# A gated attention and state-space backward pass: pool reuse waits per tile, a reordered lead-in of the channel loop, and gradient sums finished in their own tiles

## The chip, the cores and the metric

The kernel runs on one core of one Trainium2 chip. A core has five instruction streams: TensorE (PE, with its weight loads shown apart as PEld), VectorE (DVE), ScalarE (ACT), GpSimd (POOL) and SyncE (SP). SP computes nothing here: it only issues transfers, and SPq in the profile is its stream of such issues; ACT and POOL issue some too. The metric is the time of one execution on the device in microseconds (us). A run is compared by the median of its executions, and a profile is one more execution, taken with the hardware profiler on.

## The reference

The forward function mixes two branches of the same input x (2048 tokens, 576 channels) with a gate per token, and the reference returns its output and the gradients of all twelve differentiable inputs (everything but B_u):

```python
g = sigmoid((x * gate_w).sum(-1, keepdims=True))
a = softmax(q @ k.T * 18**-0.5) @ v @ wo          # 32 heads of 18, q,k,v = x @ wqkv
K = real(sum_n C * exp(dt*A*l) * (dt*B))          # per channel, 128 states, l = 0..2047
b = causal_convolution(x, K) + x * Dskip          # written with FFTs of length 4096
out = g * a + (1 - g) * b
out, vjp = jax.vjp(f, ...);  grads = vjp(grad_out)
```

So the kernel must compute attention forwards and backwards, a long convolution for each of 576 channels forwards and backwards (with the gradients of A, B, C, log_dt and Dskip), and the products that join them.

## The kernel before, in words

The program is one straight-line trace in five stages, each with its own pools of tiles:

- **Stage 1** (lines 116 to 335): loads, the q, k and v products into a DRAM tile `QKV_d`, the gradient of the attention output `dO_d`, and the parameters of the convolution `par_d`. Its last work is 160 products `ps_dO` and a row of `par_d` stores on the SP queue.
- **Attention** (lines 429 to 828). 8 groups of 4 heads, and in each 4 blocks b of 512 queries: 32 units of 32 steps, with 39 steps more at the end (`OFF`) because the backward part of a unit follows its forward part by 39 steps. A step G issues two exponentials of 128x1024 on ACT (`PT` for the forward part, `eb` for the backward part), two products `ds` of 128x512 on DVE, and on PE the score products and one burst of a gradient: V, Q and K in turn, eight steps to a round. One PSUM bank, `accB`, takes every burst and every turning of a `ds` tile (`turn`, line 553, whose eviction at line 563 is on DVE). The sums over query blocks stay in SBUF: `dvacc` and `dkacc` (four each), and `dqa`. The last addition of a sum goes to a bf16 tile `gb` (`grad_tile`, two buffers), which `store_grad` (line 529) turns with a transposing DMA on the SP queue into `gT` (two buffers); POOL packs it into `dtk` and stores it. In the last block of a group nine sums end so: four of V, four of K, one of Q. In the other blocks only the one of Q does. POOL also computes the basis `E_d` of the convolution in the gaps. The order on all engines is the order of the code (`manual_schedule`).
- **Lead-in of the channel loop** (lines 829 to 1137): tiles, constants, and the first two blocks of channels.
- **The channel loop** (lines 1138 to 1187): 18 blocks of 32 channels. For a block: `m_load`, `m_part`, `m_skw`, `m_sum`, `m_fin` form the products of short lag through a DRAM tile `Md_d` that is read back skewed; `load_en`, `turn_e` and `uv` make `UV` from the basis; `prep_rx` prepares the reversed input `RX`; `k0` and `t0_load` make the kernel's first part through a DRAM tile `Kp_d`; `scan` is the recurrence over 15 pieces on DVE, 43 dependent instructions; `rw1`, `rw2`, `t0`, `ybp` give the output; `pairs1`, `pairs2`, `sums` the parameter gradients. In iteration i, DVE scans block i while PE and ACT prepare block i + 1, and parts of blocks i + 2 and i + 3. Here PE, ACT, DVE and POOL keep the order of the code, and SP's order is chosen by the planner when the program is built.
- **Final stage** (lines 1189 to 1397): the weight gradients `ps_dwq` (320 products), the parameter gradients of the convolution (`emit_dn`), 16 token tiles with `ps_a` and `ps_dx`, and `ps_dwo`. The planner orders all of it.

A tile pool that takes over memory of an earlier pool must wait until the earlier user is done. In the kernel before this is asked of the pool as a whole: the first use of any of its tiles waits for the last use of the earlier pools that it overlaps. Within a pool, a tile of the same tag waits for the buffer that it takes.

The lines that the change touches in the lead-in:

```python
for i in range(-1, NBLK):     # 1138: iteration -1 belongs to the lead-in
    cur = i >= 0
    sb = i + 2 if i + 2 < NBLK else None
    if sb is not None:
        m_skw(sb)
```

Of the kernel before, what the change touches and what calls it, by code (L numbers as in the profile page):

```python
# [11 lines left out]
BF = mybir.dt.bfloat16  # L12
F32 = mybir.dt.float32
# [4 lines left out]
P = 128  # L18


def build(tc, aps, dbg_aps=None, stages=("s1", "attn", "post", "s4", "final")):
    nc = tc.nc
# [39 lines left out]
    with ExitStack() as gctx:  # L62
# [366 lines left out]
        if "attn" in stages:  # L429
# [5 lines left out]
            with ExitStack() as ctx:  # L435
                ctx.enter_context(tc.manual_schedule(engines={mybir.EngineType.PE, mybir.EngineType.Activation, mybir.EngineType.DVE, mybir.EngineType.Pool, mybir.EngineType.SP}))
                ga = ctx.enter_context(tc.tile_pool(name="ga", bufs=2))
                ptp = ctx.enter_context(tc.tile_pool(name="ptp", bufs=41))
                work = ctx.enter_context(tc.tile_pool(name="awork", bufs=2))
                apsp = ctx.enter_context(tc.tile_pool(name="aps", bufs=1, space=bass.MemoryType.PSUM))  # L440
                ident_f = work.tile([P, P], F32, tag="ident_f", bufs=1, name="ident_f")
# [84 lines left out]
                def grad_tile():  # L526
                    return work.tile([P, KB], BF, tag="gb", bufs=2, name="gb")

                def store_grad(gb, g, which, t0):
                    c0 = which * D + g * 4 * DH  # L530
                    gT = work.tile([P, TPQ, 4, HP], BF, tag="gT", bufs=2, name="gT")
                    nc.sync.dma_start_transpose(out=gT.rearrange("p t a b -> p t (a b)"), in_=gb)

                    def pack():
                        dtk = work.tile([P, TPQ, 4, DH], BF, tag="dtk", bufs=1, name="dtk")
                        nc.gpsimd.tensor_copy(dtk, gT[:, :, :, 0:DH])
                        nc.gpsimd.dma_start(dqkv_d[:, t0:t0 + TPQ, c0:c0 + 4 * DH], dtk.rearrange("p t a b -> p t (a b)"))
                    packs.append((now[0] + 4, pack))
# [14 lines left out]
                def turn(tiles, outs):  # L553

                    pt_ = apsp.tile([P, len(tiles), TPQ, P], BF, tag="accB", name="turn_p")
                    for x, t_ in enumerate(tiles):
                        for qb in range(TPQ):
                            nc.tensor.transpose(pt_[:, x, qb, :], t_[:, qb * P:(qb + 1) * P], ident_bf)  # L558

                    def ev():  # L560
                        x = 0
                        for n, o_ in outs:
                            nc.vector.tensor_copy(o_(), pt_[:, x:x + n])  # L563
                            x += n
                    return ev
# [31 lines left out]
                def dv_half(g, b, kq, h, acc):  # L597
                    U = UN[(g, b)]
                    for ii in (2 * h, 2 * h + 1):
                        for j in range(4):  # L600
                            mm(acc[HP * j:HP * (j + 1), :], lhsT=U["dOa"][:, ii, j, :], rhs=U["eb"].pop((kq, ii, j)),
                               start=(ii == 0), stop=(ii == 3), tile_position=(0, HP * j))

                    def ev():
                        if b == 0:
                            DKV[("v", g, kq)] = work.tile([P, KB], F32, tag="dvacc", bufs=4, name="dvacc")
                            nc.vector.tensor_copy(DKV[("v", g, kq)], acc)
                            return
                        a_ = o_ = DKV[("v", g, kq)]
                        if b == NQ - 1:  # L610
                            o_ = DKV[("v", g, kq)] = grad_tile()
                        nc.vector.tensor_tensor(o_, a_, acc, op=A.add)  # L612
                    return ev
# [19 lines left out]
                def dk_half(g, b, kq, h, acc):  # L633
# [7 lines left out]
                    def ev():  # L641
# [5 lines left out]
                        if b == NQ - 1:  # L647
                            o_ = DKV[("k", g, kq)] = grad_tile()
                        nc.vector.tensor_tensor(o_, a_, acc, op=A.add)
# [178 lines left out]
        if "s4" in stages:  # L828
            XB = 2 * CB
            GS = 16  # L830

            s4c_cm = tc.tile_pool(name="s4c", bufs=1)
            s4c = s4c_cm.__enter__()
# [6 lines left out]
            with ExitStack() as ctx:  # L840
                pc = ctx.enter_context(tc.tile_pool(name="s4l", bufs=1))
                pw = ctx.enter_context(tc.tile_pool(name="s4lw", bufs=1))
                pps = ctx.enter_context(tc.tile_pool(name="s4lps", bufs=1, space=bass.MemoryType.PSUM))
                pidx_i = pc.tile([P, 1], mybir.dt.int32, name="pidx_i")
# [12 lines left out]
                for u in range(2):  # L857
                    g_u = pc.tile([P, 2 * SUB, CB], BF, name=f"gyp{u}")
                    nc.vector.memset(g_u[:, SUB:2 * SUB, :], 0.0)
                    gyp2.append(g_u)  # L860
# [17 lines left out]

                def load_rx(xb):
                    d0 = xb * XB  # L880
                    RXn = pw.tile([P, 2 * NB, XB], BF, tag="RXn", bufs=1, name="RXn")
                    nc.sync.dma_start(RXn[:, 0:NB, :], xr_d[:, :, d0:d0 + XB])
                    nc.sync.dma_start(RXn[:, NB:2 * NB, :], gyr_d[:, :, d0:d0 + XB])
                    RXs[xb] = [RXn, None]
# [13 lines left out]

                def m_load(b):
                    xs = xss[b] = pw.tile([P, NSUB, SUB, CB], BF, tag="xs", bufs=2, name="xs")  # L900
                    src = bass.AP(tensor=xb_d.tensor, offset=xb_d[b:b + 1, 0:1, 0:1].offset,
                                  ap=[[XR * SUB * CB, NB], [SUB * CB, NSUB], [1, NSUB * SUB * CB]])
                    nc.sync.dma_start(xs.rearrange("p e t c -> p (e t c)"), src)
                    nc.sync.dma_start(gyp2[b % 2][:, 0:SUB, :].rearrange("p t c -> p (t c)"), gyb_d[b])

# [43 lines left out]

                def turn_e(b, h, q0, q1):  # L950

# [4 lines left out]
                    for q in range(q0, q1):  # L956
                        pt_ = pps.tile([P, 4, 2, N], BF, tag="bk", bufs=4, name="etp")
                        for c_ in range(4):
                            for ri in range(2):
                                nc.tensor.transpose(pt_[:, c_, ri, :], En[:, 4 * q + c_, ri, :], ident_bf)  # L960
                        nc.scalar.copy(E_[:, 4 * q:4 * q + 4], pt_)  # L961

                def load_par(b):
                    par = blk(b)["par"] = pw.tile([P, 12, CB], F32, tag="par", bufs=2, name="par")
                    nc.sync.dma_start(par, par_d[:, 0:12, b * CB:(b + 1) * CB])

                def load_en(b, h):
                    dG = b * CB + h * GS
                    En = blk(b)["En"][h] = pw.tile([P, GS, 2, P], BF, tag="E1n", bufs=6, name="E1n")
                    nc.sync.dma_start(En, E_d[:, dG:dG + GS])  # L970

# [143 lines left out]

                m_load(0)
                load_rx(0)
                load_en(0, 0)
                load_par(0)
                load_en(0, 1)  # L1120
                m_load(1)
                m_part(0, 0)
                m_part(0, 1)
                m_skw(0)
                turn_e(0, 0, 0, 2)
                prep_rx(0)
                turn_e(0, 0, 2, 4)
                m_sum(0)
                m_fin(0)
                k0(0)  # L1130
                t0_load(0)
                load_en(1, 0)
                load_en(1, 1)
                load_en(2, 0)
                load_en(2, 1)
                m_part(1, 0)
                m_part(1, 1)
                for i in range(-1, NBLK):
                    cur = i >= 0
                    nx = i + 1 < NBLK  # L1140
                    mb = i + 3 if i + 3 < NBLK else None
                    sb = i + 2 if i + 2 < NBLK else None
                    if sb is not None:
                        m_skw(sb)
# [20 lines left out]
                    if sb is not None:  # L1165
                        prep_rx(sb)
                    if cur:
                        if nx:
# [20 lines left out]
        if "final" in stages and "s4" in stages:  # L1189
# [14 lines left out]
            with ExitStack() as ctx:  # L1204
                pb = ctx.enter_context(tc.tile_pool(name="pb", bufs=1))
                pps = ctx.enter_context(tc.tile_pool(name="pps", bufs=2, space=bass.MemoryType.PSUM))
                pbw = ctx.enter_context(tc.tile_pool(name="pbw", bufs=2))
                x_tok = pb.tile([P, NT, D], BF, name="x_tok_b")
# [13 lines left out]
                with ExitStack() as actx:  # L1222
                    pf = actx.enter_context(tc.tile_pool(name="pf", bufs=1))
                    pfw = actx.enter_context(tc.tile_pool(name="pfw", bufs=2))

# [106 lines left out]

                work = ctx.enter_context(tc.tile_pool(name="pbwork", bufs=2))
                sgo = pb.tile([P, NT], F32, name="sgo")
# [109 lines left out]
```

## Time and profile before

The median of three runs is 2948.57 us (2947.92 to 2948.86). The profiled execution took 2937.9 us, and its span from the first to the last instruction is 2936.2 us; 1.7 us lie around it. Its mean granted TensorE clock is 0.923.

| stretch of the span | us | PE busy | DVE busy | ACT busy | what it is |
|---|---|---|---|---|---|
| 190.0 to 203.46 | 13.5 | 0.02 | 0.60 | 0.40 | from stage 1 to attention |
| 2050 to 2090 | 40.0 | 35.81 | 36.31 | 40.00 | a piece of attention |
| 2185 to 2195 | 10.0 | 0.00 | 0.77 | 0.00 | lead-in, first part |
| 2477.03 to 2503.96 | 26.93 | 23.26 | 25.25 | 21.10 | one iteration of the channel loop |
| 2720 to 2741 | 21.0 | 4.02 | 2.43 | 1.06 | from the loop to the final stage |
| 2805 to 2824 | 19.0 | 3.91 | 1.67 | 4.47 | inside the final stage |

Busy times of different engines overlap, and a time "idle before" an instruction is that of its engine, with the work that released it behind the arrow. An idle engine costs nothing where another one carries the stretch.

### The profile page before, as it was taken

What the parts mean: (1) busy time and instruction counts of PE and PEld (TensorE: products, weight loads), DVE (VectorE), ACT (ScalarE), POOL (GpSimd) and SP (SyncE); (2) the same over time, 40 slices, a digit from 0 to 9 for tenths busy, and PEclk for the clock granted to TensorE, in tenths of its full rate; (3) what the DMA queues carried; (4) which work ended last, traced back from release to release, by engine and by line L of the source; (5) the groups of instructions that cost most, each with busy time, mean ns of one, the idle gap of its engine ahead of it and who ended that gap; (6) DMA issues with size and microseconds to landing.
All of it is one profiled execution on the core that took longest, in us unless ns stands there. A gap on an engine that the chain in (4) does not pass through costs nothing.

```text
span 2936.2 us, 69578 instructions
## 1 busy us (share of the span) xinstructions
PE 2460.4 (84%) x27132; PEld 1182.8 (40%) x27132; DVE 2357.5 (80%) x4147; ACT 2375.9 (81%) x2792; POOL 1606.4 (55%) x2653
## 2 busy tenths in 40 slices
PE   4768988988888898898898888888866888885779
PEld 2432333332333233233333323333225878885457
DVE  4445998898898899799899989889864999999634
ACT  2449999999999999899999989999836877785111
POOL 1028888888788788787888778878210000000010
PEclk8877999999999999899999999999977888888889
DMA  8855899999989989988998998998789888882985
GB/s 224 163 152 106 157 157 171 158 164 160 170 153 167 170 153 168 168 150 161 164 168 152 166 157 156 161 173 146 130 141 263 216 222 228 214 221 63 268 195 131
DMA packets 1293343, 499.99 MB, mean 170 GB/s; under 512 B 1187774, under 2 KB 1263136, under 8 KB 1283796
## 3 DMA queue, kind: packets, MB, share of 16 engines
q1 hardware_dynamic: 1264500, 434.91, 77.1%
q0 software_dynamic: 20624, 53.26, 7.4%
q10 hardware_dynamic: 7888, 7.38, 0.8%
q8 instruction: 212, 3.47, 0.5%
q14 instruction: 119, 0.97, 0.1%
HBM read 144.48 MB, written 99.69 MB: 83 GB/s over the span
## 4 chain that ended last, share of the span: by engine, by line
ACT 34%; DVE 24%; PE 21%; DMA 8%; issue 7%; POOL 4%; SPq 3%; ACTq 0%; DVEq 0%; POOLq 0%
ACT eb L804 20%; ACT PT L799 13%; PE ps_P L30 7%; DVE ds L809 7%; DVE tz L999 4%; DVE tz L1002 3%; DVE HG L1003 2%; PE accV L30 2%; PE turn_p L558 2%; PE ps_dx L30 2%; DMA gT<-gb 2%; PE ps_dwq L30 2%; PE accK L30 2%; DVE pq L1069 1%; POOL et L358 1%
## 5 line engine op out<-in xcount | busy, mean ns | idle before, releaser
L809 DVE TENSOR_TENSOR ds<-ps_P,PT 128x512 bf16<-128x512 f32 x2048 | 1310.5, 682 | 123.2 <-PE ps_P L30 82.5
L804 ACT ACTIVATE eb<-ps_P 128x1024 bf16<-128x1024 f32 x1024 | 1098.7, 1073 | 72.1 <-PE ps_P L30 71.0
L799 ACT ACTIVATE PT<-ps_P 128x1024 bf16<-128x1024 f32 x1024 | 1102.0, 1079 | 3.2 <-PE ps_P L30 2.3
L30 PE MATMUL ps_P<-dOaT,VaT_g 32*128 32x512 bf16 x2048 | 580.6, 389 | 31.2 <-DVE ds L809 16.1
L358 POOL TENSOR_TENSOR et<-eG,eT 128x448 f32<-128x448 f32 x576 | 542.1, 961 | 10.7
L30 PE MATMUL ps_P<-QaT_g,KaT_g 32*128 32x512 bf16 x2048 | 412.9, 395 | 145.2 <-ACT PT L799 129.5
L30 PE MATMUL ps_P<-KaT_g,QaT_g 32*128 32x512 bf16 x2048 | 407.5, 391 | 2.2 <-ACT eb L804 1.6
L30 PEld LDWEIGHTS <-KaT_g 32*128 32x128 bf16 x2048 | 147.2, 91 | 480.1 <-issue 465.5
L358 POOL TENSOR_TENSOR Eo<-et,et 128x448 bf16<-128x448 f32 x288 | 327.0, 1136 | 20.8
L1105 POOL TENSOR_TENSOR SS<-m 128x96 f32<-128x96 f32 x18 | 8.9, 497 | 518.3 <-ACT m L1103 518.3
L30 PEld LDWEIGHTS <-QaT_g 32*128 32x128 bf16 x2048 | 115.9, 91 | 286.7 <-issue 265.1
L30 PE MATMUL accO<-PT,Vtok_g 128*32 128x512 bf16 x2048 | 213.2, 403 | 0.0
L30 PE MATMUL accV<-eb,dOa 128*32 128x512 bf16 x2048 | 184.6, 394 | 28.3 <-ACT eb L804 28.3
L30 PE MATMUL accK<-dsT,Qtok_g 128*32 128x256 bf16 x4096 | 166.6, 285 | 4.0 <-DMA dsT<-ds 2.4
L558 PE MATMUL turn_p<-ident_bf,ds 128*128 128x128 bf16 x1664 | 137.3, 226 | 32.1 <-DVE gb L630 31.2
L30 PE MATMUL accQ<-ds,Ktok_g 128*32 128x512 bf16 x2048 | 159.4, 389 | 2.5 <-DVE gb L612 2.1
L961 ACT COPY E1e<-etp 128x1024 bf16<-128x1024 bf16 x144 | 135.7, 1037 | 23.3 <-PE etp L960 17.7
L563 DVE COPY dsT<-turn_p 128x1024 bf16<-128x1024 bf16 (+1 forms) x224 | 143.7, 641 | 3.8 <-PE turn_p L558 3.8
L30 PEld LDWEIGHTS <-Vtok_g 128*32 128x32 bf16 x2048 | 53.6, 93 | 224.9 <-issue 224.1
L558 PEld LDWEIGHTS <-ds 128*128 128x128 bf16 x1664 | 100.4, 100 | 80.4 <-issue 80.4
L30 PEld LDWEIGHTS <-E1n 128*128 128x128 bf16 x2304 | 96.7, 109 | 87.2 <-issue 86.8
L30 PE MATMUL yp<-Rw,E1n 128*128 128x30 bf16 x1152 | 67.7, 232 | 68.7 <-DVE Rw L1024 54.2
(247 smaller groups left out, 3710.1 us busy)
## 6 DMA issues: line engine op xcount, KB each, us to landing
E_d<-Eo POOLq DMA_DIRECT2D x144, 256.0 KB, 3.7
E1n<-E_d SPq DMA_DIRECT2D x36, 1024.0 KB
xs<-xb_d SPq DMA_DIRECT2D x18, 1024.0 KB
T0w<-Kp_d SPq DMA_DIRECT2D x18, 1024.0 KB
Md_d<-mst SPq DMA_DIRECT2D x36, 288.0 KB
dsT<-ds SPq DMA_TRANSPOSE x512
dqkv_d<-dtk POOLq DMA_DIRECT2D x96, 72.0 KB, 4.4
QKV_d<-stg SPq DMA_DIRECT2D x12, 504.0 KB
```

The lines of the kernel that those rows point to most:

```text
L30: return nc.tensor.matmul(out, lhsT=lhsT, rhs=rhs, start=start, stop=stop, **kw)
L358: nc.gpsimd.tensor_tensor(out, a, b, op=op)
L558: nc.tensor.transpose(pt_[:, x, qb, :], t_[:, qb * P:(qb + 1) * P], ident_bf)
L563: nc.vector.tensor_copy(o_(), pt_[:, x:x + n])
L799: nc.scalar.activation(U["PT"][i, j // 2], ps, ACT.Exp)
L804: nc.scalar.activation(e, ps, ACT.Exp)
L809: nc.vector.tensor_tensor(U["ds"][i][:, j, :], ps, U["PT"][i, j // 2][:, j % 2, :], op=A.mult)
L961: nc.scalar.copy(E_[:, 4 * q:4 * q + 4], pt_)
L999: nc.vector.tensor_tensor(tz, HG[:, :, k - 1, :].unsqueeze(1).to_broadcast([P, 2, 4, CB]), ZZ, op=A.mult)
L1002: nc.vector.tensor_tensor(t0v, t0v, UVk[:, :, :, k, :], op=A.add)
L1003: nc.vector.tensor_tensor(HG[:, :, k, :].rearrange("p (r s) c -> p r s c", s=2), t0v, t1v[:, ::-1], op=A.add)
L1069: nc.vector.tensor_tensor(o.rearrange("p a b n c -> p a b (n c)"), a_.rearrange("p b n c -> p b (n c)").unsqueeze(1).to_broadcast([P, 2, 2 ...
```

## The change

1. **Waits per tile.** The pools of attention (`ga`, `ptp`, `awork`, `aps`), of the channel loop (`s4c`, `s4l`, a new pool `s4ld`, `s4lw`, `s4lps`) and of the final stage get `reuse_waits="tile"`: a tile waits for the earlier tiles whose bytes it takes, and not for whole pools. Stage 1's pools stay as they are. The tiles that transfers fill (`gyp`, `RXn`, `xs`, `par`, `E1n`) move into the new pool `s4ld`, ahead of `s4lw` in memory.
2. **Gradient sums.** The last addition of a V or K sum is written as bf16 over the first half of its own float32 tile (`in_place`); the transposing DMA reads it there. `gb` is left to Q and has one buffer; `gT` has three.
3. **`turn`'s eviction** is on ACT in the 39 steps after the last forward step, and on DVE as before in all others.
4. **Lead-in.** Iteration -1 is gone from the loop. The lead-in is written out in one order, for SP too; six transfers of block 0 are issued by ACT, the E evictions of block 0 are on DVE, block 0's `uv` comes before `k0`, and block 1's parts follow. Block 2's `m_part` and `m_skw` are in iteration 0, behind `prep_rx(2)`.

```diff
+ga = ctx.enter_context(tc.tile_pool(name="ga", reuse_waits="tile", bufs=2))       # and 14 more pools
...
 def grad_tile():
-    return work.tile([P, KB], BF, tag="gb", bufs=2, name="gb")
+    return work.tile([P, KB], BF, tag="gb", bufs=1, name="gb")
+def in_place(t_):
+    return t_.bitcast(BF)[:, 0:KB]
 def store_grad(gb, g, which, t0):
-    gT = work.tile([P, TPQ, 4, HP], BF, tag="gT", bufs=2, name="gT")
+    gT = work.tile([P, TPQ, 4, HP], BF, tag="gT", bufs=3, name="gT")
...
-    nc.vector.tensor_copy(o_(), pt_[:, x:x + n])
+    (nc.scalar.copy if NTOT <= now[0] < NTOT + OFF else nc.vector.tensor_copy)(o_(), pt_[:, x:x + n])
...
-    o_ = DKV[("v", g, kq)] = grad_tile()
+    o_ = DKV[("v", g, kq)] = in_place(a_)           # the same for "k"
...
-m_load(0); load_rx(0); load_en(0, 0); load_par(0); load_en(0, 1); m_load(1)
-m_part(0, 0); m_part(0, 1); m_skw(0)
-turn_e(0, 0, 0, 2); prep_rx(0); turn_e(0, 0, 2, 4)
-m_sum(0); m_fin(0); k0(0); t0_load(0)
-load_en(1, 0); load_en(1, 1); load_en(2, 0); load_en(2, 1)
-m_part(1, 0); m_part(1, 1)
-for i in range(-1, NBLK):
-    cur = i >= 0
+dve_copy = nc.vector.tensor_copy
+act_dma = nc.scalar.dma_start
+with tc.manual_schedule(engines={mybir.EngineType.SP}):
+    m_load(0, act_dma); load_en(0, 0, act_dma); load_rx(0, act_dma); load_par(0, act_dma)
+    m_part(0, 0); m_part(0, 1); m_skw(0)
+    load_en(0, 1); prep_rx(0); turn_e(0, 0, 0, 4, dve_copy); m_load(1)
+    m_sum(0); m_fin(0); load_en(1, 0)
+    uv(0, 0); turn_e(0, 1, 0, 4, dve_copy); uv(0, 1); k0(0)
+    load_par(1); prep_rx(1); m_part(1, 0); m_part(1, 1); load_en(1, 1); t0_load(0)
+    m_skw(1); turn_e(1, 0, 0, 4); m_load(2); m_sum(1); m_fin(1); load_en(2, 0); load_en(2, 1)
+for i in range(NBLK):
+    cur = True
...
-    if sb is not None:
+    if sb is not None and i > 0:
         m_skw(sb)
...
     if sb is not None:
         prep_rx(sb)
+    if i == 0:
+        m_part(2, 0); m_part(2, 1); m_skw(2)
```

(Calls that stand one to a line in the code are joined by semicolons here.)

## The prediction

> **What bounds the kernel now.** I read the busy shares in 40 slices first, then the waits of DVE and ACT in attention, then the order of time at the four places where one stage hands over to the next.
>
> No engine bounds the whole span. ACT carries attention (40.00 us busy in 40), DVE carries the channel loop. In attention the one wait that repeats is a store of a gradient:
>
> ```profile
> DVE gb L630 <- DMA gT<-gb: 34.4, 7, 7.5
> ...
> 1220.90 0.69 DVE L630 SCALAR_TENSOR_TENSOR gb<-accQ,dqa 128x512 bf16<-128x512 f32 x1 [7.47 <-DMA gT<-gb]
> ...
> 1223.24 1.02 ACT L804 ACTIVATE eb<-ps_P 128x1024 bf16<-128x1024 f32 x1 [7.09 <-PE ps_P L30]
> ```
>
> The first line is from the waits of DVE (total, times, longest). Seven times, once at each end of a group, the last Q sum finds both `gb` buffers still being turned. The two lines of the timeline show what it costs: PE waits for `accB`, and ACT, which carries the stretch, sits idle as long.
>
> The start of attention waits for its loads, and these for the end of stage 1:
>
> ```profile
> 190.89 0.45 SPq L289 DMA_DIRECT2D par_d<-t  x1
> 193.23 2.37 SPq L460 DMA_DIRECT2D KaT_g<-QKV_d  x4
> ...
> 197.95 0.58 SPq L471 DMA_DIRECT2D QaT_g<-QKV_d  x1
> ...
> 203.46 0.61 PE L30 MATMUL ps_P<-QaT_g,KaT_g 32*128 32x512 bf16 x4 [13.45 <-DMA QaT_g<-QKV_d]
> ```
>
> In the lead-in DVE is idle for 48.88 us, and the chain is one of transfers:
>
> ```profile
> 2192.35 0.58 SPq L903 DMA_DIRECT2D xs<-xb_d  x1
> ...
> 2199.98 2.10 PE L30 MATMUL psM<-xs,gyp 128*32 128x128 bf16 x32 [15.72 <-DMA xs<-xb_d]
> ...
> 2203.78 2.94 SPq L917 DMA_DIRECT2D Md_d<-mst  x2
> ...
> 2216.51 2.61 SPq L930 DMA_DIRECT2D skw<-Md_d  x4
> ...
> 2234.66 0.23 DVE L993 CAST HG<-UV 128x128 f32<-128x128 bf16 x1 [48.88 <-DMA Md_d<-mst]
> ```
>
> `xs` starts only when the last `dtk` store of attention has landed. `Md_d`, 576 KB, stands behind E1n and xs loads of 1024 KB each, and takes 12.7 us to land. Then the loop repeats every 26.93 us, and its DVE has no gap to speak of (25.25 busy, the rest between dependent instructions), so the loop itself only moves. The two hand-overs of the final stage:
>
> ```profile
> 2477.03:2503.96 26.93, 23.26 (x391) 21.94 (x389) 25.25 (x53) 21.10 (x33) 0.89 (x2) 0.88 0.87 253
> ...
> 2726.38 0.39 SPq L1209 DMA_DIRECT2D x_tok_b<-in_A_x_dram  x1
> ...
> 2741.05 13.77 PE L30 MATMUL ps_dwq<-dq_all,x_tok_b 128*128 128x426 bf16 x64 [17.03 <-DMA dq_all<-dqkv_d]
> ...
> 2819.25 3.08 SPq L1342 DMA_TRANSPOSE OT<-O_tok  x1
> ...
> 2824.37 2.56 PE L30 MATMUL ps_a<-wo_sb,OT 128*128 128x288 bf16 x10 [8.64 <-DMA OT<-O_tok]
> ```
>
> (The first is the loop iteration: PE, PEld, DVE, ACT, POOL busy, clock, DMA share, GB/s.) Loads wait at 2726 for the last `yd_d` store, and `OT` at 2819 for `dlrowb`, the last store of an unrelated pool.
>
> [...] 128x1024 bf16 out of PSUM takes 0.68 us on DVE (`dsT`) and 1.04 on ACT (`E1e`). [...] clock 0.50 from 2165 to 2195, and the first `ps_dx` of the final stage takes 3.54 us, later ones 1.88.
>
> **Part 1, gradient sums.** V and K no longer take `gb`, so Q's buffer was last used one unit earlier, 32 steps of 1979 / 1063 us, some 60 us, and its turning lands within 8 us. The seven DVE waits go. I price them by what ACT loses at the seven places: 4.35 + 4.94 + 3.28 + 7.09 + 2.78 + 6.40 + 2.79 = 31.6 us. The additions keep their 0.69 us. What is late next: the turning still stands in SP's queue behind `gT`, which waits for POOL's pack; behind it are `dsT` turnings, which PE needs some steps later. Three `gT` instead of two loosen that. A new wait is the next group's first write to the same `dvacc` or `dkacc`, 32 steps later; a turning of 8 us is covered by it. Bounds: 24 to 35.
>
> **Part 2, `turn` on ACT** in the last 39 steps. Between 2105 and 2165 DVE is busy 54.97 of 59.5 us. Eight evictions of 0.68 us and three of 0.41 leave it, about 5 us, and come to ACT at 1.04, where each step has 0.3 to 1.0 us idle. After 2165 PE at clock 0.50 carries. I take 3; bounds -1 to 5.
>
> **Part 3, start of attention.** Tiles of attention no longer wait for `par_d`'s landing: 193.23 - 191.34 = 1.9 us for sure. `QKV_d`'s last store is issued at 159, so the planner may also lift K, Q and V loads ahead of stage 1's last stores; then PE goes on at 190, and 13.5 us fall away, with a few early exponentials perhaps 16. The trace shows that the planner does lift loads past stores that come earlier in the code (a `gyp` load stands ahead of attention's last `gT`), but for a stage with a free SP order. I take the middle, 8; bounds 2 to 16.
>
> **Part 4, lead-in.** The first six loads are issued on ACT after its last `eb`, which ends at 2176.4; the last `ds`, reader of `PT` bytes below them, ends at 2176.8. `xs` took 2199.98 - 2192.35 = 7.6 us to arrive, which gives 2184.5, when PE is just through with `accK` (2184.3). So `psM` runs near 2185.5, 14.5 us earlier. `Md_d` now is first on SP; with 1.7 MB of ACT's loads in flight I give it 5 us (12.7 before, some 2.7 inside the loop), `skw` 2.7: the sums near 2196.5 against 2219.2. From there to the scan it was 15.4 us (2219.23 to 2234.66); `k0` (1.84) and block 1's `psM` (2.17) no longer stand between, and the E copies are on an idle DVE: 11.5, so the scan begins near 2208, 26.7 us earlier. Some of it is given back. Block 1's `psM` follows `k0` near 2211, its evictions follow `prep_rx(1)` (4.5) on ACT near 2215, `Md_d` lands near 2219, and `skw` is issued behind an E1n and a T0w load (2048 KB, 7.5 us at the 274 KB/us at which `x_tok` and the first piece of `dq_all`, 4012 KB, came in 14.65 us). That puts `m_fin(1)` near 2229, 21 us after the scan starts. ACT then needs 10.5 us to `hR` (2247.1 to 2257.6 before), and DVE wants `hR` 22.3 us after the start (2258.65 less its wait of 1.7): it waits about 8.5. `m_part(2)` behind `prep_rx(2)` spares PE the 5.2 + 2.2 us it stood at in iteration 0; without that the wait would be 16. Net 18; bounds 5 to 27.
>
> **Part 5, final stage.** `x_tok` lies over small tiles whose last use is two iterations before the end, and DMA is idle from 2692; it can be loaded then. `dq_all` lies over the E1n buffers, free when `ybp` ends at 2720.3. Its first piece, 1708 KB, is 6.2 us, `yd` 1.9, and 2 for landing: PE near 2731 against 2741: 10. If `x_tok` is not lifted, 4. `OT` was waiting for a whole pool; its load goes under the `ps_dwq` products. The `dqT` buffers lie over `opad` by their sizes, so `ps_dx` waits for the last turnings near 2812 and a load of 5 us: 2817 against 2828.6. I take 10. Together 20; bounds 6 to 28.
>
> **Sum.** 31.6 + 3 + 8 + 18 + 20 = 80.6 us. The profiled execution of 2937.9 becomes 2857.3. It is 10.7 us below the median of the runs; I take the same difference off the median: 2948.6 - 80.6 = 2868.
>
> **Rivals.** (a) The stores and hand-overs pay, but the lead-in gives its gain back, because DMA moved 222 to 317 GB/s there already and the same megabytes are needed, and the planner lifts nothing at the stage ends: 31.6 + 2 + 2 + 5 + 10 = 51, 2898. The DMA share near 1 in 2195 to 2215 speaks for it; the order of need against it. (b) The planner lifts much: parts 3 to 5 at their upper bounds, 31.6 + 3 + 16 + 27 + 28 = 106, 2843. (c) Waits per tile change nothing because the tiles that matter overlap late users anyway; then only the sums count, 2948.6 - 34 = 2915. (d) Slower: PE becomes the bound of attention. At clock 1.00 it is busy 45.02 us in a piece of 50 where ACT has no gap, a share of 0.90. [...] The gain of 80.6 us is 4.1% of attention's 1979 us, so the case decides where 0.90 / clock passes 1.041, at a clock of 0.865. At 0.84 the stretch is 7.2%, 142 us, longer, and the time 3010. The clock of 1.00 in the three full windows from 2000 to 2110 speaks against it.
>
> **How the numbers follow.** Main case 0.60, (a) 0.18, (b) 0.12, (c) 0.06, (d) 0.04. A difference under 0.2%, 6 us, is about what runs of this kernel can't tell from none. The main case alone spans 2853 to 2885. From 2838 to 2908 the range holds the main case, (b) and (a), save their tails: about 8 in 10. Faster 0.95, same 0.01, slower 0.04.
>
> **What would show it.** Right: no DVE wait of L630 on `gT<-gb`; ACT gaps of 3 to 7 us gone at the seven ends of groups; the first `psM` within 3 us of the last `accK`; the first scan less than 30 us after it, and one DVE wait for `hR` in iteration 0; loop iterations still 26.9; `ps_dwq` within 12 us of the last `yp`; `OT` turned while `ps_dwq` runs. Wrong: a new wait of equal size at `dvacc` or `dkacc`, SP standing at a lifted load while `dsT` is due, or DVE starving in iterations 1 and 2 as well.

## The result, and the profile after

The changed kernel takes 2931.35 us in the median of four runs (2922.88 to 2937.84) where the kernel before takes 2948.24 (2943.93 to 2948.86): a ratio of 0.9944, with a 95% interval of 0.9917 to 0.9971. A second comparison gave 2925.17 against 2942.45, 0.9945 (0.9926 to 0.9964). So the change is worth about 17 us, 0.6%, where 80.6 us were predicted. The direction was right; the size was wrong by a factor of nearly five, and the time lies above 2908, the upper end of the range.

The profiled execution of the changed kernel took 2931.12 us with a span of 2929.4, only 6.8 us below the 2936.2 of the kernel before: the profiled execution of before was 10.3 us faster than its median, that of after is at its median. (`PT` and `eb` are the exponentials of the forward and the backward part of attention, the scan is DVE's recurrence of a block.) Stretch by stretch, measured between the same instructions in both traces:

| stretch | before, us | after, us | change | predicted |
|---|---|---|---|---|
| to the first `PT` (part 3) | 205.5 | 201.2 | -4.3 | -8 |
| first to last `PT` (part 1) | 1899.1 | 1893.8 | -5.3 | -31.6 |
| last `PT` to last `eb` (part 2) | 70.8 | 72.8 | +2.0 | -3 |
| last `eb` to the scan of block 3 (part 4) | 141.5 | 150.8 | +9.3 | -18 |
| from there to the last `ybp` (`yp`) products | 399.9 | 400.1 | +0.2 | 0 |
| from there to `ps_dwq` (part 5) | 24.3 | 22.3 | -2.0 | -10 |
| `ps_dwq` to the end (part 5) | 195.2 | 188.4 | -6.8 | -10 |

A second trace of the changed kernel has -4.1, -8.8, +3.9, +5.8, +0.8, -2.1 and -6.0 in the same rows, so every sign repeats. Three readings carry the table.

**Attention.** The waits from 205 to 2150 us (total, times, longest), of the kernel before:

```profile
ACT eb L804 <- PE ps_P L30: 60.2, 53, 7.1
...
PE turn_p L558 <- DVE gb L630: 30.4, 7, 6.9
...
PE accK L30 <- DMA dsT<-ds: 2.4, 3, 1.6
```

and of the changed kernel, where no line of L634, the former L630, waiting for a `gT` is left:

```profile
ACT eb L808 <- PE ps_P L30: 52.8, 56, 5.8
...
DVE dkacc L653 <- PE accK L30: 32.5, 69, 6.2
...
PE accK L30 <- DMA dsT<-ds: 24.9, 9, 5.6
```

PE stood 32.8 us for `gb` and `dsT` together and now stands 24.9 for `dsT`; ACT, which carries the stretch, has got back only 7.4 us.

The end of the fourth group, the place that the prediction showed at 1220.90, in the timeline of the changed kernel:

```profile
1221.71 1.04 PE L30 MATMUL accK<-dsT,Qtok_g 128*32 128x256 bf16 x16 [5.56 <-DMA dsT<-ds]
...
1222.81 0.69 DVE L653 TENSOR_TENSOR dkacc<-dkacc,accK 128x512 bf16<-128x512 f32 x1 [6.21 <-PE accK L30]
...
1223.34 1.02 ACT L808 ACTIVATE eb<-ps_P 128x1024 bf16<-128x1024 f32 x1 [5.84 <-PE ps_P L30]
```

The wait has changed its cause, not its place. DVE no longer waits for a `gT` that is being turned; PE waits 5.56 us for a `dsT` that is being turned, and ACT still loses 5.84 us where it lost 7.09.

**Lead-in.** The timeline of the changed kernel: the last loads and turnings of attention, the first products and the first scan, then what iterations 0 and 1 wait for:

```profile
2168.24 0.62 ACTq L908 DMA_DIRECT2D xs<-xb_d  x1
2168.69 2.20 SPq L821 DMA_TRANSPOSE dsT<-ds  x1
...
2185.70 1.04 PE L30 MATMUL accK<-dsT,Qtok_g 128*32 128x256 bf16 x16 [9.75 <-DMA dsT<-ds]
2186.53 2.18 PE L30 MATMUL psM<-xs,gyp 128*32 128x128 bf16 x32
...
2210.70 0.23 DVE L998 CAST HG<-UV 128x128 f32<-128x128 bf16 x1 [1.70 <-ACT UV L991]
...
2230.21 0.60 PE L30 MATMUL misc<-sel,skw 128*128 128x8 f32 x2 [10.76 <-DMA skw<-Md_d]
...
2245.46 2.23 DVE L1074 TENSOR_TENSOR pq<-UV,hR 128x1920 bf16<-128x1920 bf16 x2 [12.45 <-ACT hR L1015]
...
2267.60 0.60 PE L30 MATMUL misc<-sel,skw 128*128 128x8 f32 x2 [9.88 <-DMA skw<-Md_d]
...
2272.62 2.16 DVE L1023 TENSOR_TENSOR wa<-HG,par 128x1920 f32<-128x1920 f32 x1 [7.10 <-PE misc L30]
```

The first scan does start 24.2 us after the first `psM` and 24.0 us earlier than before (16.5 counted from the last `eb`, since attention ended 7.5 us earlier). But the last `accK` waits 9.75 us for a `dsT` turning that was issued among ACT's loads, and the skewed reads of blocks 1 and 2 (`skw`) arrive 20 and 57 us after the first scan. The same trace in windows from scan to scan (length; PE, PEld, DVE, ACT, POOL busy; clock, DMA share, GB/s):

```profile
2210.70:2249.75 39.05, 24.31 (x373) 21.97 (x373) 25.10 (x52) 20.05 (x31) 0.00 (x0) 0.65 0.91 213
2249.75:2291.72 41.97, 28.05 (x452) 26.30 (x450) 25.43 (x54) 23.04 (x35) 3.04 (x2) 0.80 0.68 185
2291.72:2318.62 26.90, 23.12 (x394) 21.91 (x392) 25.22 (x53) 23.77 (x36) 0.87 (x2) 0.90 0.90 224
```

DVE has the same 25 us of work in each, so iteration 0 loses 12 us and iteration 1 15 us. In the kernel before they were 28.3 and 26.9 us long.

**Final stage.**

```profile
2722.94 0.56 SPq L1071 DMA_DIRECT2D yd_d<-yd  x1
2723.60 3.39 SPq L1230 DMA_DIRECT2D x_tok_b<-in_A_x_dram  x1
...
2741.04 4.42 PE L30 MATMUL ps_dwq<-dq_all,x_tok_b 128*128 128x426 bf16 x12 [15.10 <-DMA dq_all<-dqkv_d]
...
2815.42 2.58 PE L30 MATMUL ps_a<-wo_sb,OT 128*128 128x288 bf16 x10
...
2823.74 0.82 DVE L1384 SCALAR_TENSOR_TENSOR o0b<-dif,g_t,y_b 128x576 bf16<-128x576 f32 x1 [4.95 <-DMA out_dram<-dlrowb]
```

`x_tok` still stands behind the last `yd_d` store in SP's queue. `OT` is turned early (at 2791.34, under the `ps_dwq` products), and `ps_a` comes 9 us earlier than before, but the first `o0b` waits 4.95 us for the store of `dlrowb`, whose bytes it takes.

### The profile page after: what moved, and what is told of

It reads as the page before. It is cut to its first block, busy times and chain, and to the rows that moved or that the text cites. A ratio compares the mean times of both kernels' runs of the same rounds, so it can differ in the third digit from the quotient of the medians.

```text
span 2929.4 us, 69534 instructions
## 1 busy us (share of the span) xinstructions
PE 2479.6 (85%) x27132; PEld 1190.7 (41%) x27132; DVE 2359.5 (81%) x4146; ACT 2376.7 (81%) x2793; POOL 1611.4 (55%) x2653
## 5 line engine op out<-in xcount | busy, mean ns | idle before, releaser
L803 ACT ACTIVATE PT<-ps_P 128x1024 bf16<-128x1024 f32 x1024 | 1096.6, 1073 | 14.0 <-PE ps_P L30 12.8
L30 PE MATMUL accK<-dsT,Qtok_g 128*32 128x256 bf16 x4096 | 164.9, 283 | 36.6 <-DMA dsT<-ds 34.6
L966 ACT COPY E1e<-etp 128x1024 bf16<-128x1024 bf16 x136 | 128.0, 1034 | 16.2 <-PE etp L965 16.1
L30 PEld LDWEIGHTS <-Qtok_g 128*32 128x32 bf16 x4096 | 88.6, 97 | 102.0 <-issue 65.7
```

Source lines behind the costliest of these rows:

```text
L30: return nc.tensor.matmul(out, lhsT=lhsT, rhs=rhs, start=start, stop=stop, **kw)
L803: nc.scalar.activation(U["PT"][i, j // 2], ps, ACT.Exp)
```

## The experiments

Ratios are to the kernel before on the same chip, with their 95% intervals. Its medians there were 2941.18 us (first four kernels: e1, e3, e4, e5), 2942.45 (next four: the changed kernel, e9, e10, e8) and 2940.01 (last four: e2, e6, e7, e11). A ratio is estimated from all runs of both sides and can differ from that of the medians, most for e10 (0.9872 against 0.9855). Differences from the changed kernel of 0.003, 9 us, are just clear of the noise or at its edge, and are read together with the traces.

### The changed kernel again

> The changed kernel itself, as the reference for the runs beside it. Every theory expects the ratio to the kernel before at 0.992 to 0.997, as in its first comparison, and DVE waits of about 27 us in iterations 0 and 1.

Measured: 2925.17 us, 0.9945 (0.9926 to 0.9964), with 26.2 us of DVE waits for `hR` and `misc` in iterations 0 and 1. This is the reference for the experiments below; e1 to e11 are their names.

### Attention: where the gain of the sums went

**The sums alone (e1).**

```diff
 # the kernel before, with in_place(), gb bufs=1 and gT bufs=3; everything else unchanged
-    o_ = DKV[("v", g, kq)] = grad_tile()
+    o_ = DKV[("v", g, kq)] = in_place(a_)      # the same for "k"
```

> The kernel before with the gradient sums alone (V and K finished in their own tiles, one gb, three gT); pools, lead-in and turn as before. The prediction: ACT's seven gaps of 3 to 7 us close, 31.6 us (24 to 35) are gained, the last eb starts near 2144 instead of 2175.4. Transfer theory (the DMA engines are full at the ends of groups, so the wait only passes from DVE's gb to PE, which waits for dsT): the waits of L630 for gT are 0, but PE's waits for dsT rise from 2 us to 20 or more, the gaps of ACT stay at five or more of the eight places, and the gain of attention is 3 to 8 us.

Measured: 2929.54 us, 0.9964 (0.9952 to 0.9977). First to last `PT` 1894.5 us, 4.6 less than before; last `eb` at 2170.43. No wait of L634 for a `gT`, and in PE's waits from 205 to 2150 us:

```profile
PE accK L30 <- DMA dsT<-ds: 19.7, 11, 4.2
```

That is what the transfer theory expected (19.7 us where it said 20 or more, 4.6 us gained where it said 3 to 8). The gain of Part 1 is lost in this edit itself, not in its company: PE's 32.8 us of waits for `gb` and `dsT` become 19.7 for `dsT`, and ACT's waits for `ps_P` fall from 60.2 to 53.1 us and no further.

**Scattering stores moved (e3).** POOL's stores `put_x`, `put_gy` and `put_zero` fill the layouts `xb_d` and `gyb_d` of the convolution during attention.

```diff
-at(("pre", 216 + 56 * r), lambda r=r: put_zero(r))
-at(("pre", 78 + 56 * k), lambda k=k: put_x(k)); at(("pre", 98 + 56 * k), lambda k=k: put_gy(k))
+# the next of the steps 52, 64, ... 112 of every 128, in the same order
+at(("pre", next(slots_)), lambda r=r: put_zero(r))
+at(("pre", next(slots_)), lambda k=k: put_x(k)); at(("pre", next(slots_)), lambda k=k: put_gy(k))
```

> The kernel after, with the 39 scattering stores of POOL (put_x, put_gy, put_zero) and the first row of Kp_d moved to steps 52 to 112 of each 128, away from the ends of the groups; same bytes, same number. Transfer theory (what PE waits for at the ends of groups is a share of full DMA engines): PE's waits for dsT before 2160 fall from 25 us to 12 or less, the gaps of ACT shrink most at 1223 and 1706, and the last eb starts 6 to 15 us earlier than 2167.9. Queue theory (dsT is late because SP's queue is in order and stands at gT, whatever else moves): PE's waits for dsT stay within 5 us of 34.6 and the last eb starts within 3 us of 2167.9.

Measured: 2914.83 us, 0.9908 (0.9893 to 0.9923). First to last `PT` 1868.5 us, last `eb` at 2150.40, and in PE's waits from 205 to 2150 us:

```profile
PE accK L30 <- DMA dsT<-ds: 9.0, 8, 2.0
```

The last `eb` is 17.5 us earlier than in the changed kernel, more than the 6 to 15 that were expected. SP's queue holds the same transfers in the same order; only POOL's moved. So it is not the order on SP alone that makes `dsT` late: what is sent at that time from elsewhere counts.

**K and V sums copied, not turned (e2).** This kernel leaves out the turning of the K and V gradients, so it is of use for its times alone.

```diff
+    if which:
+        nc.sync.dma_start(gT.rearrange("p t a b -> p (t a b)"), gb)
+    else:
         nc.sync.dma_start_transpose(out=gT.rearrange("p t a b -> p (t a b)"), in_=gb)
```

> The kernel after, with the K and V sums copied into gT by a plain transfer instead of a transposing one (8 of the 9 turnings of a group's last unit; the K and V gradients are then not turned, so the products that use them compute something else). Tile order, waits and SP's places are the same. Transfer theory (the turnings take their time from full DMA engines, and the dsT turnings behind them come late): PE's waits for dsT before 2150 fall from 17 to 25 us to 10 or less, and from the first to the last PT it takes 1865 to 1875 us instead of 1880 to 1894. Buffer theory (SP stands in order until POOL has packed a gT, whatever fills it): the waits stay at 15 us or more and the stretch at 1880 or more.

Measured: 2909.41 us, 0.9894 (0.9881 to 0.9908). First to last `PT` 1868.0 us, and in the same view:

```profile
PE accK L30 <- DMA dsT<-ds: 7.0, 2, 4.1
```

The buffer theory falls: the copies go through the same `gT` buffers and POOL packs, and the waits go down with the turnings. Each of the two edits alone leaves a rival: a copy also takes SP less time to issue (0.54 us in the median, a turning of `dvacc` or `dkacc` 1.25), and e3 frees POOL as well. But e3 leaves SP's transfers as they are and e2 leaves POOL's; what both change is what the DMA engines are given at the ends of groups, and both bring the stretch to 1868 us. That the engines have less to do there is not shown by their busy share: from 1200 to 1230 us it is 1.01 in the changed kernel and 1.06 in e3, and from 300 to 2100 us 0.934 in the changed kernel (with 290 MB) and 0.926 in e2 (with 293). So load as the cause is an inference from the two edits. Nine traces with the changed kernel's own attention program in this stretch (the changed kernel twice, e4 to e10) lie between 1879.6 and 1893.8.

One thing more goes down with these waits. Between 270 us and the last `PT`, PE spends 72 us at clock 0.50 in the kernel before, 68 in the changed one, 27 in e3 and 20 in e2, always in spells of 3 to 17 us that begin within 30 us of the end of a group. So the ends of groups also go with time at half clock; the runs don't part what that costs from the wait itself.

**`turn` on DVE throughout (e7).**

```diff
-(nc.scalar.copy if NTOT <= now[0] < NTOT + OFF else nc.vector.tensor_copy)(o_(), pt_[:, x:x + n])
+nc.vector.tensor_copy(o_(), pt_[:, x:x + n])
```

> The kernel after, with the eviction of turn on DVE in the last 39 steps too. The prediction: the stretch from the last PT to the last eb is 3 us longer (-1 to 5) than in the kernel after, where it was 70.5 to 77.3. Null theory (in these steps PE at half clock and the transfers set the pace, and ACT gets three eights of a 1.04 us copy more to do): it is 69 to 71 us, as in the two kernels with the eviction on DVE (70.8 and 69.5), and the time within 4 us of the kernel after.

Measured: 2919.49 us, 0.9938 (0.9916 to 0.996), which the time can't tell from the changed kernel. From the last `PT` to the last `eb` it is 68.2 us. With the eviction on DVE the three traces have 68.2 to 70.8, with it on ACT the eleven others have 70.5 to 77.7. But the length of this stretch follows PE's granted clock in it, almost without exception in the fourteen traces: from 68.2 us at 0.90 (e7) to 77.7 at 0.58 (e2). At nearly the same clock the two places are alike: 70.8 us at 0.80 on DVE (before), 70.5 at 0.81 on ACT (e5). So no gain of Part 2 is to be seen. The three traces with DVE have the higher clocks (0.80 to 0.90, the others 0.58 to 0.81); whether the move to ACT lowers the clock is not settled.

### Lead-in: what the new order costs

All of these are read from the last `eb`, since the attention before it varies by some us from run to run:

| kernel | last sum of `accK` after last `eb` | first `psM` | first scan | iteration 0 | iteration 1 | scan of block 3 |
|---|---|---|---|---|---|---|
| before | 8.9 | 24.6 | 59.3 | 28.3 | 26.9 | 141.5 |
| changed | 18.9 | 18.7 | 42.8 | 39.1 | 42.0 | 150.8 |
| e4, lead-in of before | 9.0 | 13.8 | 51.5 | 28.6 | 26.9 | 134.1 |
| e5, other order on SP | 13.8 | 13.5 | 37.9 | 36.8 | 39.0 | 140.5 |
| e9, e5 and block 2 earlier | 21.2 | 20.9 | 44.5 | 38.5 | 27.1 | 137.1 |
| e6, first loads on SP | 9.0 | 12.8 | 36.8 | 39.2 | 38.8 | 141.8 |
| e10, e9 with two edits more | 7.9 | 14.3 | 39.2 | 31.5 | 34.2 | 131.8 |
| e11, with e3 and e8 | 9.0 | 12.7 | 36.8 | 31.2 | 34.6 | 129.5 |

**The lead-in of before, in the changed kernel (e4).**

```diff
 # tile waits, sums, turn as in the changed kernel; the written-out lead-in is replaced by the one of before
-for i in range(NBLK):
-    cur = True
+for i in range(-1, NBLK):
+    cur = i >= 0
```

> The kernel after, with the lead-in of the kernel before (iteration -1, all loads on SP, E copies on ACT, block 2's short-lag products in the lead-in, SP's order left to the planner there); everything else as after. The prediction: 18 us (5 to 27) slower than the kernel after. Give-back theory (the 24 us by which the first scan is earlier are lost again in iterations 0 and 1, because block 1's and 2's transfers come no earlier): the first scan starts about 24 us later after the last accK, DVE waits under 4 us in iterations 0 and 1 instead of 27.5, and the time is within 6 us of the kernel after.

Measured: 2909.93 us, 0.9887 (0.9868 to 0.9907), against 0.9945 (0.9926 to 0.9964) for the changed kernel. Both theories on record were too kind to the new lead-in: undoing it makes the kernel about 17 us faster (0.9945 less 0.9887, times 2941), and its trace has 16.7 us of that between the last `eb` and the scan of block 3. The scans of blocks 0 and 1 in DVE's timeline:

```profile
2214.54 0.23 DVE L998 CAST HG<-UV 128x128 f32<-128x128 bf16 x1 [41.52 <-ACT UV L991]
2243.11 0.22 DVE L998 CAST HG<-UV 128x128 f32<-128x128 bf16 x1
```

Tile-wise waits alone let the old order start its loads earlier: `psM` runs 13.8 us after the last `eb` instead of 24.6, and nothing is given back in the loop, 7.4 us gained up to block 3. The new order reaches the first scan 8.7 us sooner than that and then loses 10.5 and 15.1 us.

**Other places in SP's order (e5).**

```diff
     m_skw(0); load_en(0, 1)
-    prep_rx(0); turn_e(0, 0, 0, 4, dve_copy); m_load(1); m_sum(0); m_fin(0); load_en(1, 0)
+    m_load(1); load_en(1, 0); load_par(1); m_load(2); load_en(1, 1)
+    prep_rx(0); turn_e(0, 0, 0, 4, dve_copy); m_sum(0); m_fin(0)
...
-    load_par(1); prep_rx(1); m_part(1, 0); m_part(1, 1); load_en(1, 1); t0_load(0)
-    m_skw(1); turn_e(1, 0, 0, 4); m_load(2); m_sum(1)
+    prep_rx(1); m_part(1, 0); m_part(1, 1); m_skw(1); t0_load(0)
+    turn_e(1, 0, 0, 4); m_sum(1)
```

> The kernel after, with other places in SP's order of the lead-in only: xs(1), E1n(1,0), par(1), xs(2) and E1n(1,1) are issued right behind E1n(0,1), ahead of Kp_d(0), and skw(1) stands directly behind Md_d(1), ahead of T0w(0). Order theory (SP stands at the Kp_d store from 2201 to 2213 while the DMA engines are 0.26 to 0.59 busy, and skw(1) stands behind three loads): the first scan stays within 2 us of 2210.7, block 1's sums come near 2222 instead of 2230 to 2233, DVE's wait for hR in iteration 0 falls from 12.5 to 4 or less, and 8 to 15 us are gained. Megabyte theory (the same bytes are needed, DMA is full and no order helps): the loop's end stays within 4 us, since each load that goes ahead delays Md_d(1) or skw(1) as much.

Measured: 2915.32 us, 0.9913 (0.9899 to 0.9927), some 9 us faster than the changed kernel, but not by what was expected: iteration 0 still waits 10.2 us for `hR`. The sums of block 1 come 18.7 us after the first scan instead of 19.5. The planner had placed the loop's `xs(3)` between `Md_d(1)` and `skw(1)`, and the read was issued 8.5 us after its store. About half of the gain in the table is the earlier last `accK` (13.8 us after the last `eb` instead of 18.9), which this edit doesn't touch. Taken alone this run decides little.

**Block 2 back in the lead-in (e9).**

```diff
 # e5, and:
     turn_e(1, 0, 0, 4)
+    m_part(2, 0); m_part(2, 1); m_skw(2)
     m_sum(1)
...
-    if i == 0:
-        m_part(2, 0); m_part(2, 1); m_skw(2)
```

> e5_order with one thing more: block 2's m_part and m_skw go back from iteration 0 into the lead-in, behind turn_e(1, 0) and ahead of m_sum(1). Order theory (in iteration 0 they stand behind uv(1, 1) on PE and prep_rx(2) on ACT, so skw(2) is issued 48 us after the first scan, and iteration 1 waits for m_sum(2)): iteration 1 falls from 39 to about 28 us, iteration 0 stays at 35 to 38, and the kernel is 8 to 12 us faster than e5_order. Megabyte theory (DMA was full in these stretches and sets the end): iterations 0 and 1 together stay within 4 us of the 76 of e5_order, the time moves by less than 4 us. The prediction's words (m_part(2) behind prep_rx(2) spares PE 7.4 us of standing in iteration 0) would make it slower.

Measured: 2909.24 us, 0.989 (0.9868 to 0.9912). The scans of blocks 1 and 2:

```profile
2240.98 0.22 DVE L998 CAST HG<-UV 128x128 f32<-128x128 bf16 x1
2268.09 0.22 DVE L998 CAST HG<-UV 128x128 f32<-128x128 bf16 x1
```

Iteration 1 is 27.1 us, 11.8 less than in e5, as the order theory had it. So the move of block 2's products into iteration 0 is what starves iteration 1. The kernel is some 7 us faster than e5, where 8 to 12 were expected: up to block 3 only 3.4 us are kept, because in this run the last `accK` came 7.4 us later than in e5. The megabyte theory falls for iteration 1, and the prediction's opposite sign with it.

**The first six loads on SP (e6).**

```diff
-act_dma = nc.scalar.dma_start
+act_dma = nc.sync.dma_start
```

> The kernel after, with block 0's first six loads on SP, in its fixed order behind the last gT, instead of on ACT. Collision theory (ACT's loads of 2.5 MB start before the last dsT turning and delay it): the last accK comes 9 to 10 us after the last eb, where it took 14 to 21 us with the loads on ACT; xs arrives later in exchange, the first psM comes 16 to 20 us after the last eb, and the time is within 5 us of the kernel after. Rival (the last dsT is late for the gT turnings ahead of it on SP): the last accK stays at 14 us or more, psM moves to 22 or more, and it is 4 us slower or more.

Measured: 2917.48 us, 0.9916 (0.9901 to 0.993), about 9 us faster than the changed kernel, more than the 5 that were expected. The last `accK` and the first `psM` of PE, whose last `eb` started at 2164.07:

```profile
2171.10 1.90 PE L30 MATMUL accK<-dsT,Qtok_g 128*32 128x256 bf16 x32 [0.85 <-DVE dsT L567]
2176.86 2.18 PE L30 MATMUL psM<-xs,gyp 128*32 128x128 bf16 x32 [3.86 <-DMA gyp<-gyb_d]
```

The 9.75 us wait for the last `dsT` is gone. In the table the last sum of `accK` comes after 7.9 to 9.0 us where the loads are on SP, and after 13.8 to 21.2 where they are on ACT, so the collision is shown. And `psM` doesn't run later in exchange, as I had expected, but 6 us earlier: starting the loads early on another queue had brought nothing, since PE's order put `psM` behind the `accK` that they delayed.

**Block 1's products first, loads on SP outside the fixed order (e10).** Two loads of the lead-in, `m_load(2)` and `load_en(1, 1)`, also move behind block 1's products, and `prep_rx(1)` behind `t0_load(0)`.

```diff
 # e9, and: the first loads stand ahead of the fixed SP order, on nc.sync
-    m_load(1); load_en(1, 0); load_par(1); m_load(2); load_en(1, 1)
+    m_load(1); load_en(1, 0); load_par(1)
...
     uv(0, 1)
-    k0(0); prep_rx(1); m_part(1, 0); m_part(1, 1); m_skw(1); t0_load(0)
+    m_part(1, 0); m_part(1, 1); m_load(2); m_skw(1); load_en(1, 1)
+    k0(0); t0_load(0); prep_rx(1)
```

> e9_part2 with two things more: m_part(1) stands ahead of k0(0) and prep_rx(1), and block 0's first loads are on SP, outside the fixed order, instead of on ACT. Order theory: Md_d(1) leaves about 6 us earlier, iteration 0 is 30 to 33 us instead of 37; with the loads off ACT the last accK comes within 9 to 11 us of the last eb (13 to 20 with the loads on ACT, 8.9 before), and the first psM 13 to 15 us after the last eb. From the last eb to the scan of block 3: 120 to 128 us, against 151 in the kernel after, 141 before and 134 with the lead-in of before. Megabyte theory: it stays at 134 or more.

Measured: 2899.84 us, 0.9872 (0.9847 to 0.9898). Iteration 0 is 31.5 us as expected, `psM` comes as expected, and `accK` a little sooner. But iteration 1 is 34.2 us, and block 3 is reached after 131.8, between the two theories. What is late now is, by the longest wait, another transfer, block 2's `RXn` (waits from 2194 to 2288; it was issued behind two `E1n` loads of 1024 KB each):

```profile
ACT RX L898 <- DMA RXn<-gyr_d: 12.9, 2, 10.3
```

So the new order of transfers, with the loads off ACT, is worth about 19 us against the changed kernel (150.8 less 131.8). That what is left is a queue of loads is argued, not shown: the DMA engines are 0.98 and 0.93 busy up to the second scan. Against the plain old lead-in (134.1) little is won.

### The final stage

```diff
-    nc.sync.dma_start(yd_d...[:, :, x0:x0 + XB], yd...)
+    (nc.scalar if b == NBLK - 1 else nc.sync).dma_start(yd_d...[:, :, x0:x0 + XB], yd...)
...
-    rowb = pf.tile([1, D], BF, name="dlrowb")
+    rowb = pb.tile([1, D], BF, tag="dgwb", name="dlrowb")
```

> The kernel after, with the last yd store issued by ACT instead of SP, and the row dlrowb in the buffer of dgwb (pool pb) instead of in pf. Queue theory of the last stage (x_tok and dq_all wait only because they stand behind that store on SP, and o0b of the first token tile waits for dlrowb's store because it takes its bytes): x_tok is issued more than 15 us before the last ybp ends, ps_dwq starts 12 us or less after it instead of 18.7, DVE's 5 us wait for dlrowb is gone, and 10 to 15 us are gained. Rival (dq_all needs the E1n buffers and its 1.7 MB set the start): ps_dwq starts 15 us or more after the last ybp, and only up to 5 us are gained.

Measured: 2914.19 us, 0.9912 (0.9893 to 0.9931), about 10 us faster than the changed kernel, at the lower end of what was expected. SP's queue, then PE:

```profile
2674.97 0.39 SPq L1230 DMA_DIRECT2D x_tok_b<-in_A_x_dram  x1
2716.98 2.48 SPq L1249 DMA_DIRECT2D dq_all<-dqkv_d  x2
...
2725.17 5.13 PE L30 MATMUL ps_dwq<-dq_all,x_tok_b 128*128 128x426 bf16 x14 [4.93 <-DMA dq_all<-dqkv_d]
```

With that one store out of its way, `x_tok` is issued 38 us before the last `ybp` products start, and `ps_dwq` starts 8.2 us after they end (at 2716.95) instead of 18.7. The prediction's size for this step was right; what it took for granted, that the planner would lift the load, was not. The wait for `dlrowb` is gone too, but its removal gains nothing: from the first `ps_dwq` to the end this kernel takes 189.1 us, the changed one 188.4 and 189.2. Here the first `ps_a` comes 78.9 us after the first `ps_dwq` instead of 74.4; PE waits 4.1 us for ACT's evictions of `ps_dwq`, where it waited 0.3. So the whole gain is that of `x_tok`.

### Everything together

e3, e10 and e8 in one kernel (the edits shown above).

> The edits of e3_puts, e10_lead and e8_final together. If their gains stand in different stretches they add: e3 took 0.37% off the kernel after, e10 0.73%, e8 0.33%, so the ratio to the kernel before is 0.9945 - 0.0143 = 0.980, about 2884 us against 2942. If the shares of transfers collide (the lead-in gets its loads only when the attention's transfers are done), e3's part is lost again and the ratio is 0.984.

Measured: 2885.05 us, 0.9815 (0.9801 to 0.9828). The gains add but for 0.13 of 1.43%, and this version is 55 us below the kernel before and about 38 below the changed one. Its trace is a warning about single stretches: PE's waits for `dsT` are 10.0 us as in e3, but from the first to the last `PT` it takes 1875.3 us and not 1868.5.

## Why the prediction was wrong

**Part 1, gradient sums, failed by 26 us, the largest term.** No DVE wait for a `gT` is left, as was said. The step that failed is the pricing: "I price them by what ACT loses at the seven places". That takes the whole stall for the wait's own; of the 31.6 us ACT got back 7.4. The text named what is late next, the `dsT` turnings behind `gT` in SP's queue, let "three `gT`" answer it and gave it no time. It was nearly as late as `gb`: 4.6 us are gained in e1 and 5.3 in the change. That the cause is load, not buffers, is inferred from e2 and e3 together: from 300 to 2100 us the DMA queues took 81.3 + 11.5 + 0.6 = 93% of the 16 engines' time, and both edits shorten the stretch to 1868 us by changing what is sent at the ends of groups, where SP's order and the buffers stay.

**Part 4, lead-in, had the wrong sign: 18 us predicted, 9.3 lost.** Three terms make the 27 us. First, 10 us up to the first scan, which came 42.8 us after the last `eb` where the prediction has 32.6: ACT's loads delayed the last `dsT`, so `accK` ended 18.9 us after the last `eb` and not 8.9, and `psM` ran behind it. (Taking the loads off ACT gives 6 of the 10 us back, in e6.) The prediction counted on `xs` arriving "when PE is just through with `accK`" and did not ask what those loads pass on the way. That they slow SP's turnings, as e6 shows (last sum of `accK` 9.0 us after the last `eb` with these loads on SP, 18.9 with them on ACT), has no place in it. Second, 15 us: iteration 1. The prediction costed block 1 through iteration 0 and stopped; `m_part(2)` behind `prep_rx(2)` was booked as a relief for PE, and e9 shows that it costs 12 us. Third, 2 us: iteration 0 became 10.8 us longer and not 8.5, where the mechanism was right and only its size was off. And one gain was not seen at all: waits per tile let the old lead-in's loads start earlier as well (e4), worth 7.4 us without any new order. The comparison that mattered was new order against old order with the same waits.

**Part 5, final stage, 8.8 of 20 us.** `ps_dwq` had 10 us to win and e8 wins them. The failed step: "it can be loaded then". The tiles were free, but the planner kept `x_tok` behind the last `yd_d` store. The 2 us for landing were an estimate: the quickest stores in the trace of before, `obo`, land 1.7 us (16 KB) and 2.3 us (128 KB) after their issue. In the second half the mechanism was right and the size a little off: `ps_a` did come 9 us earlier, and 6.8 of the 10 us were left at the end. The new tile wait of 4.95 us, `o0b` on `dlrowb`, was not foreseen, but e8 removes it and gains nothing in this half, so what keeps the rest is open.

**Part 3, start, 4.3 of 8 us,** within its bounds: the loads left 3.1 us earlier (`KaT` at 190.16 instead of 193.23), close behind the last `par_d` store, and none was lifted ahead of stage 1's stores. Some 1.4 us of the gain are another's: ACT's table load of 1.28 us, which stood behind the load of `Vtok_g` at 204.22, now runs at 189.28. **Part 2** was put at 3 us and brought none that can be seen: +2.0 and +3.9 us in the two traces go with a lower clock (0.73 and 0.68, before 0.80). Two readings of the prediction bear on this. The durations 0.68 us on DVE and 1.04 on ACT are whole durations at one width, and as such they price the move (in the changed kernel a `dsT` of that width takes 1.01 us on ACT). And the clock of 0.50 from 2165 began while PE was busy, 9.58 of the 10 us to 2175; what brought it about is not shown.

**Rivals.** (a) was the nearest in kind, "the lead-in gives its gain back" and "the planner lifts nothing", but it kept Part 1 whole. (c) was near in time and wrong in mechanism: tile waits do work (e4), and the sums pay little. (b) is out: the loads that it counts on at the ends of stage 1 and of the loop were not lifted. (d) is out: the clock from 205 to 2095 us is 0.97 in both kernels, with PE busy 1671.7 us of that before and 1685.1 after. That PE's time goes about as 1 / clock, as (d) reckons, is in the trace of before (`ps_dx` groups of 14 products take 3.54 us at clock 0.50, 2.63 at 0.71 and 1.88 at 1.00); its clock of 0.84 was the author's assumption. Of the signs set down beforehand for being wrong, two appeared: a new wait of nearly equal size (DVE's 32.5 us at `dkacc`, of which 8.2 were there before, where 34.4 at `gb` had gone), and DVE starving in iteration 1 as well. Three signs for being right appeared too (`psM` right behind `accK`, the scan less than 30 us after it, loop iterations of 26.9 us) and say little about the time. That the kernel is faster at all was forecast for a sum in which one term has the wrong sign: the gains of parts 1, 3 and 5 outweigh the loss of part 4.

## What to carry to other kernels

When a wait is removed, price what the same stretch still needs, and from whom: here, with the DMA engines busy 0.93 of the time, the next transfer in line was nearly as late as the one whose wait had gone, and what gained was a plain transfer in place of a turning (PE's waits from 24.9 to 7.0 us), or stores at another time (to 9.0). Before judging a new order, put the old order under the same new waits. And an earlier start is worth only what the second and third iterations can keep: follow each later block's longest chain of transfers until the loop is steady.

## What the runs showed of the hardware that was not expected

A plain transfer in place of a transposing one of the same tile took away most of PE's waiting (24.9 to 7.0 us) though it is only eight transfers per group. Moving POOL's stores, with every turning left, did nearly as much (9.0 us), so the runs don't say that a turning is dearer than other load. Loads issued by ACT made a turning issued by SP at the same time late: PE waited 9.75 us for the last `dsT` with `xs` and `E1n` in flight from ACT, and with the same loads behind it on SP (e6) it stood 0.85 us before its last `accK`, for DVE. PE's clock fell to 0.50 in spells of 3 to 17 us at the ends of groups, and the length of attention's last stretch went with the clock in it (68.2 us at 0.90, 77.7 at 0.58). The same attention program took 1879.6 to 1893.8 us in nine traces, more than several of the effects that were to be told apart; readings within one trace, from one landmark to the next, were needed beside the medians.
